# A transformer block's lead-in with three attention jobs' exponentials kept in SBUF, and seven units' second-norm transposes made by DMA

## The chip, the cores and the metric

The kernel runs on one core of a Trainium2 chip. A core has TensorE (PE; the load of its stationary operand is listed as PEld), VectorE (DVE), ScalarE (ACT), GpSimd (POOL) and SyncE (SP, which here only issues DMAs). Times are device microseconds of one execution. The time before is 1102.87 us, the median of three runs (1101.98 to 1104.28). In the profile, L12 is line 12 of the kernel before.

## The reference

A pre-norm transformer block on x of 2048 rows and 1024 columns in bf16, with 32 heads of 32 columns and a hidden layer of 3584. A layer norm here has no scale or shift.

```python
def _A_ref(x, wqkv, wo):
    B, S, D = x.shape
    H = 32; Dh = D // H
    qkv = (lambda x, *d: x.transpose(*d))((x @ wqkv).reshape(B, S, 3, H, Dh), 2, 0, 3, 1, 4)
    q, k, v = qkv[0], qkv[1], qkv[2]
    scale = Dh ** -0.5
    scores = jnp.einsum("bhqd,bhkd->bhqk", q, k) * scale
    p = _softmax(scores, axis=-1)
    o = jnp.einsum("bhqk,bhkd->bhqd", p, v)
    return (lambda x, *d: x.transpose(*d))(o, 0, 2, 1, 3).reshape(B, S, D) @ wo

def _B_ref(x, w1, b1, w2, b2):
    h = jnp.einsum("bsd,df->bsf", x, w1) + b1
    h = _gelu(h)
    return jnp.einsum("bsf,fd->bsd", h, w2) + b2

x = A_x
h = x + _A_ref(_layernorm(x, axis=-1), A_wqkv, A_wo)
h2 = h + _B_ref(_layernorm(h, axis=-1), B_w1, B_b1, B_w2, B_b2)
```

## The kernel before

**A planner writes the order.** The program first makes a list of tasks (`Graph.add`, L84). Each task has an engine, an occupation in us, a latency, a priority, and the buffers that it reads and writes, from which its dependences follow. `Graph.schedule` (L109) then plays the list through with these figures and writes down, for each engine, the order in which the tasks start. `assign` puts semaphores on what is left of the dependences and `emit` writes the instructions. On the chip every engine goes through its own list in that order and waits where a semaphore is not there yet. The planner's figures (L487 to L559: `MM`, `c_dve_ps`, `c_dve`, `c_act`, and the occupations and latencies in the calls) thus set the order and nothing else.

For TensorE `pick_pe` (L1144) chooses among the ready tasks by kind: scores (`qk`) go first; a value product (`pv`) or a denominator (`den`) is taken once `PV_FORCE` = 3 of them are ready, or when there is nothing else; otherwise the background work (`bg`) goes in the order of the list; `warm` is taken when there is nothing to do at all. On the other engines the task with the lowest priority number goes first.

**Attention.** The 32 heads are 8 groups g of four heads (128 columns). A job is one block qb of 256 query rows with one group g. It has eight rounds r of 256 keys. A round is: scores (`Att.qk`, L769: eight matmuls on quarters of the array's rows), two exponentials on ACT of 128x1024 elements (L779) from PSUM into one of nine buffers of `PT`, a sum of two halves on DVE into `PS` (L820), the value product (`Job.pv`, L805) and the denominator, a product with ones (`Job.den`, L834). The scores use PSUM in units of two banks; `n_units` says how many there are (three are banks 0 to 5). A job collects its output in one bank and `Job.finish` (L850 to L865) divides and stores it in `OT`.

**Order of the whole.**
- The lead-in: chunk hc of eight, two row tiles of 128 rows each, is loaded, normalized on DVE (`layer_norm`, L583 to L598), transposed by TensorE (L604) and copied from PSUM to `xnT` (L611 on ACT for most tiles, L613 on DVE). Then K of group 0 (and, for the first two chunks, Q) and V of groups 0 and 1 (`proj_v`, cast in L706) for that chunk, and rounds of jobs (0,0) and (1,0) with `n_units` 2 and a lag of two rounds. Banks 4 and 7 take the background work there, 5 and 6 the two jobs' outputs. In these two jobs the denominators are made from `PT` directly, without the DVE sum.
- For g = 1 to 7: Q, K and the next groups' V projections (`rest_of_projections`, L1072) as background, and jobs (0,g) and (1,g); for g = 2 (`EXTRA`) also (2,g).
- Then the remaining jobs, block by block, with this background for unit u = 0 to 6 (a unit is 256 rows): output projection `wo` (L886), second layer norm `ln2` (L914), first FFN layer `ffn1` (L925) with the GELU in `gelu` (a tanh on ACT, L965), second FFN layer `ffn2` (L969). The order within a unit is `wo(u + 1)`, `ffn2(u, 0)`, `ln2(u + 1)`, `ffn2(u, 1)`, `ffn1(u + 1)`. Banks 6 and 7 go to background work and job outputs.
- The tail: unit 7's output projection, norm and FFN, behind the last job.

At the start 80 `warm` matmuls (L1007) write bank 6. In `ln2`, each of the two tiles is normalized into `xb` (L598), transposed by eight matmuls into a PSUM bank (L604) and copied to `hnT` (L613; by ACT, L611, in the tail). The call is:

```python
            transposes(R.xb[:, s, :], R.B_xb[s], slot(), hnT[:, :, t * P:(t + 1) * P], B_hnT[t],
                       "act" if tail else "dve", 0)
```

All DMAs are issued by SP, in the planner's order. Weights come into rings: four blocks of 512 KB for the first layer (`w1r`), seven for the second (`w2r`).

## Time and profile before

| what | value |
|---|---|
| median of three runs | 1102.87 us |
| the profiled execution, first to last instruction | 1099.2 us |
| TensorE busy (its ends are modelled) | 1056.5 us |
| ACT busy | 1019.8 us, of which 1024 exponentials (L779) 953.6 |
| DVE busy | 757.2 us |
| transposes by TensorE outside the tail (L604) | 128 for xnT, busy 9.7 us; 112 for hnT, busy 9.0 us |
| copies to hnT by DVE (L613) | 14, 9.4 us |
| copies to xnT by ACT (L611) | 12, 12.2 us |
| DMA share over the span, main queue | 51.2% |

The profiled execution is one run of its own; its span counts from its first to its last instruction and lies 3.7 us under the median of the timed runs. A busy time is the union of an engine's instructions. "Idle before" is the time an engine stood still just before a group of instructions, with what released it. The chain that ended last is followed back from the last instruction, at each step to what released it or to the instruction before it on its engine.

### The profile page before, as it was taken

The page shows a single profiled execution, that of the slowest core. Times are in us where ns is not written, and L with a number is a line of the kernel's source. Part 1 is how long each engine was busy: PE and PEld are TensorE (multiplying, and loading weights), DVE is VectorE, ACT ScalarE, POOL GpSimd, SP SyncE. Part 2 cuts the span into 40 slices and gives each one's busy share as a digit, 9 for nine tenths or more (in the row PEclk, how much of TensorE's full clock was granted, in tenths as well). Part 3 has the DMA queues.
Part 4 walks back from the last instruction along what each step waited for, and adds up shares of the span by engine and source line. Part 5 has one row for each costly group of instructions (what it writes and reads, how often), then busy time and mean ns, then how long its engine had stood idle before and what let it go on. Part 6 is the DMA issues. An engine that isn't in the chain of part 4 may idle for free.

```text
span 1099.2 us, 42056 instructions
## 1 busy us (share of the span) xinstructions
PE 1056.5 (96%) x19177; PEld 613.8 (56%) x19226; DVE 757.2 (69%) x1444; ACT 1019.8 (93%) x1124; POOL 47.8 (4%) x110
## 2 busy tenths in 40 slices
PE   8899999998899999999999899999999999999998
PEld 6655555553345744664475456546744664565483
DVE  7746666665676886788588768876886787687501
ACT  3879999999999999999999999999999999999650
POOL 3200000000000001001000100010010000000100
PEclk9999999999899999999999999999999999999999
DMA  6820000048345654854576466448654747797370
GB/s 184 227 103 2 29 2 3 2 159 268 115 122 154 189 151 150 260 162 149 185 228 188 150 203 180 143 150 255 181 178 149 216 142 239 243 266 242 98 262 20
DMA packets 265506, 174.43 MB, mean 159 GB/s; under 512 B 26864, under 2 KB 260336, under 8 KB 264560
## 3 DMA queue, kind: packets, MB, share of 16 engines
q1 hardware_dynamic: 265328, 171.74, 51.2%
q8 instruction: 151, 2.47, 0.9%
q14 instruction: 27, 0.22, 0.1%
HBM read 161.23 MB, written 10.49 MB: 156 GB/s over the span
## 4 chain that ended last, share of the span: by engine, by line
ACT 79%; PE 19%; DVE 1%; issue 0%; DMA 0%; POOL 0%; POOLq 0%; DVEq 0%
ACT PT L779 75%; PE ps L540 6%; ACT uu L965 4%; PE ps L537 4%; PE ps L534 3%; PE ps L769 2%; PE ps L805 1%; PE ps L1007 1%; PE ps L834 1%; DMA a_w1r<-in_A_wo_dram 0%; ACT xnT L611 0%; PE ps L604 0%; DVE PS L820 0%; DVE OD L850 0%; DVE OD L857 0%
## 5 line engine op out<-in xcount | busy, mean ns | idle before, releaser
L779 ACT ACTIVATE PT<-ps 128x1024 bf16<-128x1024 f32 x1024 | 953.6, 1189 | 18.2 <-PE ps L769 18.0
L820 DVE TENSOR_TENSOR PS<-PT 128x1024 bf16<-128x1024 bf16 x434 | 287.5, 686 | 124.5 <-ACT PT L779 63.8
L769 PE MATMUL ps<-QT,KT 32*128 32x256 bf16 x4096 | 204.6, 273 | 13.5 <-ACT PT L779 10.2
L805 PE MATMUL ps<-PT,V 128*32 128x256 bf16 x4096 | 179.9, 273 | 1.5 <-ACT PT L779 1.1
L769 PEld LDWEIGHTS ps<-QT,KT 32*128 32x128 bf16 x4096 | 61.0, 92 | 174.1 <-ACT PT L779 165.3
L834 PE MATMUL ps<-PS,ones 128*32 128x256 bf16 x1736 | 121.7, 274 | 2.0 <-DVE PS L820 2.0
L805 PEld LDWEIGHTS ps<-PT,V 128*32 128x32 bf16 x4096 | 103.8, 97 | 30.0 <-issue 8.7
L537 PE MATMUL ps<-a_w2r,gT 128*128 128x512 bf16 x445 | 109.6, 380 | 4.9 <-issue 2.4
L537 PE MATMUL ps<-hnT,a_w1r 128*128 128x256 bf16 x903 | 111.2, 273 | 1.1 <-DVE rr L860 0.5
L534 PE MATMUL ps<-hnT,a_w1r 128*32 128x256 bf16 x2660 | 96.9, 274 | 2.4 <-DVE gT L943 1.2
L537 PEld LDWEIGHTS ps<-hnT,a_w1r 128*128 128x128 bf16 x903 | 82.7, 98 | 25.1 <-issue 14.8
L943 DVE TENSOR_TENSOR gT<-ps,b1f 128x512 bf16<-128x512 f32 x98 | 67.3, 687 | 27.7 <-PE ps L534 18.4
L534 PE MATMUL ps<-a_w2r,gT 128*32 128x512 bf16 x1140 | 81.6, 381 | 2.5 <-DVE OD L857 2.5
L534 PEld LDWEIGHTS ps<-hnT,a_w1r 128*32 128x32 bf16 x2660 | 66.2, 96 | 18.5 <-issue 14.0
L537 PEld LDWEIGHTS ps<-a_w2r,gT 128*128 128x128 bf16 x471 | 40.4, 98 | 55.3 <-issue 15.7
L989 DVE SCALAR_TENSOR_TENSOR hch<-ps,hch 128x512 bf16<-128x512 f32 x32 | 22.0, 689 | 64.0 <-PE ps L540 47.1
L834 PEld LDWEIGHTS ps<-PS,ones 128*32 128x32 bf16 x1736 | 45.9, 96 | 22.8 <-issue 8.7
L965 ACT ACTIVATE uu<-uu 128x1024 bf16<-128x1024 bf16 x49 | 58.0, 1206 | 0.0
L537 PE MATMUL ps<-xnT,Wall 128*128 128x512 bf16 (+1 forms) x213 | 47.7, 360 | 2.3 <-issue 1.1
L588 POOL CAST mvb<-mv 128x2 bf16<-128x2 f32 (+1 forms) x25 | 6.1, 242 | 990.0 <-DVE mv L585 987.2
L706 DVE CAST V<-ps 128x512 bf16<-128x512 f32 x32 | 22.1, 690 | 30.8 <-PE ps L537 15.8
L537 PE MATMUL ps<-Wall,xnT 128*128 128x256 bf16 x327 | 41.0, 273 | 0.0
(85 smaller groups left out, 1009.8 us busy)
## 6 DMA issues: line engine op xcount, KB each, us to landing
a_w2r<-in_B_w_dram SPq DMA_DIRECT2D x105, 512.0 KB, 5.6
a_w1r<-in_B_w_dram SPq DMA_DIRECT2D x98, 512.0 KB, 4.4
a_w1r<-in_A_wo_dram SPq DMA_DIRECT2D x32, 512.0 KB, 4.0
b_w1r<-in_B_w_dram SPq DMA_DIRECT2D x14, 512.0 KB, 5.8
a_w1r<-in_A_wqkv_dram SPq DMA_DIRECT2D x11, 512.0 KB, 4.3
xrb<-in_A_x_dram SPq DMA_DIRECT2D x16, 256.0 KB, 4.2
Wall<-in_A_wqkv_dram SPq DMA_DIRECT2D x16, 256.0 KB, 4.8
hch<-in_A_x_dram SPq DMA_DIRECT2D x16, 256.0 KB, 4.0
```

Of the source, the lines that this page charges most:

```text
L534: fns.append(lambda p, j=j: p.matmul(psum[32 * j:32 * j + 32, bi(bank), c0:c1], lhsT[:, 32 * j:32 * j + 32], rhs, start=start, stop=stop, ...
L537: t.whole = lambda p: p.matmul(psum[:, bi(bank), c0:c1], lhsT, rhs, start=start, stop=stop, skip_group_check=True)
L540: t = pe(lambda p: p.matmul(psum[:, bi(bank), c0:c1], lhsT, rhs, start=start, stop=stop), occ, reads=reads, writes=[bb(bank)], mode="full" ...
L706: t = dve(lambda v: v.tensor_copy(dst, psum[:, bi(bank), :].rearrange("p (t g c) -> p g t c", t=2, g=2)), c_dve_ps(512), reads=[bb(bank)], ...
L769: return p.matmul(psum[:, 2 * us[h // 2] + h % 2, 256 * i:256 * i + 256], KT[32 * h:32 * h + 32, g, k0:k0 + P], QT[32 * h:32 * h + 32, qs, :],
L779: act(lambda a, u=u, k=k: a.activation(PT[:, s, k, :, :], psum[:, 2 * u:2 * u + 2, :], ACT.Exp, bias=0.0, scale=SCALE), 1024, reads=[B_ps[ ...
L805: fns.append(lambda p, i=i, h=h: p.matmul(psum[32 * h:32 * h + 32, bi(bank), 0:256], V[:, g, 2 * r + i, 32 * h:32 * h + 32], PT[:, s, h // ...
L820: dve(lambda v: v.tensor_tensor(PS[:, n, :, :], pairs[:, :, 0:256], pairs[:, :, 256:512], ALU.add), c_dve(1024, 2), reads=[B_PT[2 * s], B_ ...
L834: fns.append(lambda p, h=h, rhs=rhs, i=i: p.matmul(psum[32 * h:32 * h + 32, bi(bank), 256:512], ones32[:, :], rhs, start=False, stop=last, ...
L943: t = dve(lambda v: v.tensor_tensor(g[:, fc:fc + 2, :], psum[:, bi(bank), :].rearrange("p (f c) -> p f c", f=2), b1f[:, fc:fc + 2].unsquee ...
L965: act(lambda a: a.activation(w, w, ACT.Tanh, bias=0.0, scale=KT2), 1024, reads=[B_uu[i]], writes=[B_uu[i]], prio=-1)
L989: drop(dve(lambda v, hs=hs, bank=bank, half=half: v.scalar_tensor_tensor(hch[:, hs, c], psum[:, bi(bank), :], half, hch[:, hs, c], ALU.mul ...
```

## The change

Four things change together.

1. **The lead-in.** Scores and exponentials of three jobs, (0,0), (1,0) and (2,0), run in the lead-in (`NLJ = 3`), with three units from the start. Their 24 rounds of exponentials each get a buffer of their own: eight of the nine of `PT` are used, and 16 more (`extra_pt`) lie over memory that is not yet in use there (K and V of groups 2 to 5, V of group 1, three of the weight blocks, and a piece behind them). V of group 0 is projected after all of this (`proj_v1`, four times four tiles), and the value products of the three jobs come behind it: the planner counts none of them as ready until the last cast of that V (`gate`) is done. They use the DVE sum as all others do, and those sums come after the last DVE task of the lead-in (`hold`). ACT copies only tiles 0 to 3 to `xnT`; DVE copies the other twelve. All background work uses banks 6 and 7, bank 6 from the end of the warm matmuls on. V of group 1 is projected in the stage g = 1.
2. **One more extra job.** `EXTRA` is now (1, 2), and the loops behind it follow.
3. **The second layer norm's transposes** of units 0 to 6 are made by one DMA for each tile of 128x1024, from `xb` to `hnT`, both in SBUF, issued by SP. Unit 7 keeps TensorE and ACT.
4. **The planner's figures** for matmuls, DVE and ACT instructions, latencies and switches are others.

The loads of V's weights are cut differently: 128 columns at first, behind the first eight row tiles, and the other 384 in one piece later.

```diff
+    PTs = [PT[:, i] for i in range(NR)]
+    B_PTs = [B_PT[2 * i:2 * i + 2] for i in range(NR)]
...
+    def extra_pt(off):
+        i = len(PTs)
+        h, b = sb(Area(off), "PX%d" % i, [P, 2, 2, 512], BF, 2)
+        PTs.append(h)
+        B_PTs.append(b)
+
+    for g in (2, 3, 4, 5):
+        extra_pt(B_KT[8 * g].lo)
+        extra_pt(B_V[NT * g].lo)
+    for k in (5, 3, 1):
+        extra_pt(B_W[k][0].lo)
+        extra_pt(B_W[k][0].lo + 4096)
+    extra_pt(ph0.cur)
+    extra_pt(B_V[NT].lo)
...
-    MM = 0.2195
+    MM = 0.21333
     def c_dve_ps(n):
-        return (120 + n) / 960.0 + 0.02
+        return (120 + n) / 960.0 - 0.058
 
     def c_dve(n, x=1):
-        return (62 + n / x) / 960.0 + 0.085
+        return (62 + n / x) / 960.0
...
     def pe(fns, occ, reads=(), writes=(), kind="bg", mode="full", prio=0, after=()):
-        return gr.add(E.PE, fns, occ, 0.16, reads, writes, prio, kind, mode, after)
+        return gr.add(E.PE, fns, occ, 0.225 if isinstance(fns, list) and len(fns) > 1 else 0.2, reads, writes, prio, kind, mode, after)
...
     def lead_slot():
-        s = Slot(gr.buf(), 1, (4, 7))
-        s.buf.over.append(B_ps[4])
-        B_ps[4].over.append(s.buf)
-        lead_slots.append(s)
-        return s
+        return slot()
...
+    def dma_transpose(out_ap, in_ap, nbytes, reads, writes, prio):
+        return gr.add(E.SP, lambda s: s.dma_start_transpose(out_ap, in_ap), 0.06, 0.0, reads, writes, prio, nbytes=2 * nbytes)
...
-            transposes(R.xb[:, s, :], R.B_xb[s], slot(), hnT[:, :, t * P:(t + 1) * P], B_hnT[t],
-                       "act" if tail else "dve", 0)
+            if tail:
+                transposes(R.xb[:, s, :], R.B_xb[s], slot(), hnT[:, :, t * P:(t + 1) * P], B_hnT[t], "act", 0)
+            else:
+                dma_transpose(hnT[:, :, t * P:(t + 1) * P], R.xb[:, s, :], P * 2048, [R.B_xb[s]], [B_hnT[t]], -1)
...
-            if r == 7 or (self.g == 0 and self.qb < 2):
+            if r == 7:
                 self.sums.append((s, True))
...
-    load_w(WV, -5, 0, 256)
     for tt in range(4, 8):
         x_tile(tt, -5)
+    load_w(WV, -5, 0, P)
     for k in range(80):
-        pe(lambda p: p.matmul(psum[:, 6, 0:256], ident[:, :], b2t[:, 0:256], start=True, stop=True), 0.12,
+        pe(lambda p: p.matmul(psum[:, 6, 0:256], ident[:, :], b2t[:, 0:256], start=True, stop=True), 0.18 if k < 42 else 0.115,
            reads=[B_ident, B_b2t], writes=[B_ps[6]], kind="warm")
-    LEAD_LAG = 2
-    lead_jobs = [Job(0, 0, 6), Job(1, 0, 5)]
-
-    att.n_units = 2
+    LEAD_ACT = (0, 1, 2, 3)
+    NLJ = 3
+    last_x = []
...
-            tr_tile(tt, lead_slot(), "dve" if tt >= 8 and tt % 2 else "act")
+            tr_tile(tt, slot(), "act" if tt in LEAD_ACT else "dve")
...
+        if hc < NLJ:
+            proj_half(0, hc, slot(), ev)
+        proj_half(1, hc, slot(), ev)
         if hc < 7:
             lead_norm(hc + 1)
-        proj_v(2 * hc, 0, lead_slot(), ev, first)
-        for k, r in {0: [(0, 0)], 1: [(0, 1), (1, 0), (1, 1)]}.get(hc, [(0, hc), (1, hc)]):
-            s = att.qk((k, 0), r)
-            pending.append((lead_jobs[k], r, s))
-            attention_drain(LEAD_LAG)
-    attention_drain()
-    att.n_units = 3
-    att.unit = 0
-    N_LEAD = sum(t.kind == "pv" for t in gr.tasks)
-    pool_banks = {4: [], 7: [], 6: [t for t in gr.tasks if any(t in x.w or t in x.r for x in (B_ps[6], B_psD[6]))]}
+        for k, r in [(k, hc) for k in range(min(hc, NLJ))] + ([(hc, r) for r in range(hc + 1)] if hc < NLJ else []):
+            n = 8 * k + r
+            s = NR + 15 if n == 0 else n - 1 if n < 9 else n
+            lead_rounds.append((k, r, att.qk((k, 0), r, s)))
+    att.rounds = 8
+    hold = [t for t in gr.tasks if t.eng == E.DVE][-1:]
+    for c in range(4):
+        proj_v1(4 * c, 0, 4, slot(), "dve", 0, True)
+    gate = gr.tasks[-1]
+    for k in range(NLJ):
+        job = Job(k, 0, slot(2))
+        for _, r, s in [x for x in lead_rounds if x[0] == k]:
+            job.pv(r, s)
+    pool_banks = {6: [t for t in gr.tasks if t.kind == "warm"][-1:], 7: []}
...
+        if g == 1:
+            for c in range(4):
+                proj_v1(4 * c, 1, 4, slot(), "dve", 0, True, [gate])
+        if g in EXTRA:
+            proj(0, g, 1, slot(), "dve")
...
-    EXTRA = [2]
+    EXTRA = [1, 2]
     for g in range(1, G):
         rest_of_projections(g)
-        if g in EXTRA:
-            proj(0, g, 1, slot(), "dve")
+        if g == 2:
+            proj(0, 0, 1, slot(), "dve")
...
-    attention(2, [g for g in range(G) if g not in EXTRA])
+    attention(2, [g for g in range(1, G) if g not in EXTRA])
...
+        if gate.done is None or gate.done > now + 1e-9:
+            return 0
...
-        if pv_next[0] < N_LEAD:
-            waiting += PV_FORCE - 1
```

More of the change, by code (lines that the diff above doesn't have):

```diff
@@ L708, in proj_v, with proj_v1 @@
         drop(t, bank)
-    def proj_v1(tt, g, n, bank, evac, c0=0):
+    def proj_v1(tt, g, n, bank, evac, c0=0, narrow=False, after=()):
         for k in range(n):
@@ L715, in proj_v1 @@
                 mm(bank, xnT[:, tc, dc, t4 * P:(t4 + 1) * P], Wall[4][:, dc, P * g:P * g + P], dc == 0, dc == DC - 1,
[L716 removed]
+                   [B_W[4][g], B_xnTt[tc][t4]], narrow, cols=(c0 + P * k, c0 + P * k + P), after=after)
         dst = V[:, g, tt:tt + n, :]
@@ L754, in __init__, with qk @@
             self.jobs = 0
-        def qk(self, job, r):
+        def qk(self, job, r, s=None):
             qb, g = job
@@ L849, in finish @@
             D = OD[:, o, 1, :].rearrange("p (b j) -> p b j", j=32)
-            t = dve(lambda v: v.transpose(OD[:, o, 1, :], psum[:, bi(bank), 256:512]), 0.445,
+            t = dve(lambda v: v.transpose(OD[:, o, 1, :], psum[:, bi(bank), 256:512]), 0.36,
                     reads=[self.B_O, self.B_D], writes=B_D, prio=-1)
@@ L1097, in build_kernel @@
             attention(2, [g])
-    for g in range(2):
+    for g in range(1, 2):
         if g not in EXTRA:
@@ L1126, in build_kernel @@
     pvs = [t for t in gr.tasks if t.kind == "pv"]
-    pv_exp = [[d for d in t.deps if d.eng == E.Activation and d.kind == "exp"] for t in pvs]
+    pv_exp = [[d for d in t.deps if d.eng == E.Activation and d.kind == "exp" or d.eng == E.DVE] for t in pvs]
     pv_next = [0]
@@ L1146, in pick_pe @@
         spare = None
+        ready_rounds(now)
         n67 = sum(b > 5 for b in free)
```

58 lines of the change are left out of this document (27 added, 31 removed).

## The prediction

> **What bounds the kernel now.** I read the page first, then the busy time by stage, then what ScalarE (ACT) waited for in the lead-in and behind it, then ACT's instructions in order of time. The page:
>
> ```profile
> PE 1056.5 (96%) x19177; PEld 613.8 (56%) x19226; DVE 757.2 (69%) x1444; ACT 1019.8 (93%) x1124; POOL 47.8 (4%) x110
> ...
> ACT 79%; PE 19%; DVE 1%; issue 0%; DMA 0%; POOL 0%; POOLq 0%; DVEq 0%
> ```
>
> Two engines look full. TensorE's 96% is modelled, and the chain that ended last runs through ACT for 79% of the span. By stage (width, then busy time and count of PE, PEld, DVE, ACT, POOL, then the clock and the DMA share):
>
> ```profile
> 24.80:71.21 46.41, 42.03 (x1032) 29.43 (x1033) 29.75 (x67) 35.88 (x38) 7.95 (x17) 1.00 0.70 201
> 71.21:279.50 208.29, 200.09 (x3674) 111.09 (x3687) 129.50 (x234) 208.29 (x228) 0.00 (x0) 1.00 0.20 65
> ...
> 1031.00:1099.20 68.20, 64.77 (x434) 40.29 (x439) 11.49 (x23) 19.43 (x37) 3.40 (x8) 1.00 0.37 125
> ```
>
> From 71.2 on ACT is busy without a break: 228 exponentials in 208.29 us, 0.914 us each. The last one ends at 1031.1; the 68.1 us behind it are TensorE's (the last unit's output projection and two FFN layers). So the time is the moment at which ACT becomes continuous, plus ACT's remaining work, plus 68. ACT's waits, in the lead-in (16 to 72 us) and then from 71 to 1031:
>
> ```profile
> ACT PT L779 <- PE ps L769: 15.0, 12, 3.8
> ...
> ACT PT L779 <- PE ps L769: 6.7, 5, 3.6
> ```
>
> Behind 71 us only 6.7 us are to be had from ACT; in the lead-in there is more:
>
> ```profile
> 24.82 1.02 ACT L779 ACTIVATE PT<-ps 128x1024 bf16<-128x1024 f32 x1 [3.82 <-PE ps L769]
> 25.73 2.85 ACT L611 ACTIVATE xnT<-ps 128x1024 bf16<-128x1024 bf16 x3
> ...
> 57.58 1.94 ACT L779 ACTIVATE PT<-ps 128x1024 bf16<-128x1024 f32 x2 [0.55 <-PE ps L769]
> 60.09 1.94 ACT L779 ACTIVATE PT<-ps 128x1024 bf16<-128x1024 f32 x2 [0.58 <-PE ps L769]
> 63.12 1.94 ACT L779 ACTIVATE PT<-ps 128x1024 bf16<-128x1024 f32 x2 [1.08 <-PE ps L769]
> 65.63 1.94 ACT L779 ACTIVATE PT<-ps 128x1024 bf16<-128x1024 f32 x2 [0.57 <-PE ps L769]
> 71.21 4.69 ACT L779 ACTIVATE PT<-ps 128x1024 bf16<-128x1024 f32 x5 [3.65 <-PE ps L769]
> ```
>
> Every pair of exponentials waits about 0.55 us: the lead-in uses two PSUM units, a round fills both, so the next round's scores (L769) cannot be written until this round's are read. Besides, ACT copies normalized tiles (L611), and at 71.2 it waits 3.65 us for the next group's first projections.
>
> **The lead-in.** By 71.21 ACT has done 32 exponentials. Between 24.8 and 71.2 it did 30 of them, eight L611 copies (8 x 1.03 = 8.2 us) and was idle for 46.41 - 35.88 = 10.5 us. The change takes all three causes away: only tiles 0 to 3 are copied by ACT, scores go round three units, and 24 rounds (48 exponentials) are on offer before group 1 is needed. If ACT runs without a break from the second chunk's first exponential, which I put at 24.0 (24.8 before; V's eight-matmul fillers and a V cast are gone ahead of it, but the 80 warm matmuls now hold bank 6 until the last has run), the 33rd starts at 24.0 + 30 x 0.914 = 51.4. That is 19.8 us before 71.21 (10.5 idle, 8.2 copies, 0.8 start, rounding). Bounds for the start: 22 (two tiles' copies right behind each other) to 27 (one bank serialises the second chunk, three copies of 1.0 more).
>
> Can it be fed? VectorE (DVE) has, over the lead-in, 21.2 us of L583, 3.3 of L585 (16 of 32), 8.0 of L598, 1.1 of L589, twelve xnT copies at 0.69 = 8.3, and ten casts of 128x256 at 0.42 = 4.2: 46 us from 3.4 on, done near 50. The seven later chunks offer 3, 5, 3, 3, 3, 3, 3 rounds, so ACT wants chunk 7 only at 24 + 20 rounds x 1.83 = 60.6, chunk 2 at 29.5 (before, its K cast came at 28.8 with V casts in between). TensorE per chunk: 16 transposes (1.0 us), eight to sixteen 256-wide matmuls (0.9 to 1.8), three rounds (0.33 each): under 4 us of 5.5. So ACT sets the pace, and I book 19.8.
>
> **The handover, at a cost of 2 us.** V of group 0 (64 narrow 128-column matmuls, 3.6 us, and four casts of 0.69) and all 24 value products come after the scores, behind the gate (the last V cast), near 53. They cost TensorE 24 x (0.22 + 0.11) = 8 us and DVE 21 sums x 0.69 = 14.5 us, while group 1's first Q and K (16 matmuls, 3.5 us, two casts) must be there at 66 to 68, when ACT has used up its 24 rounds. The planner prefers a value product as long as three are ready, so the projections stand behind that burst unless they were fitted in before; their weights landed at 33 to 35 us before, so mostly they can be. Nothing hidden: 0; hidden by nothing: the 8 us of the burst. I take 2. The loads of the second halves of W wait for the third job's value products, about 75 us, and are wanted beyond 110: no cost. Score rounds of group 1 write buffers that job 0's products must have read; those run first.
>
> **One more Q projection and 16 more rounds ahead of group 2.** ACT's total stays. TensorE gets 8 x 0.219 us earlier. Two jobs' sums now go through DVE (14 x 0.69) and TensorE saves 14 x 0.11 = 1.5 us. Nothing on the path: DVE is 69% busy.
>
> **The planner's figures.** They move the order, not a duration. With ACT's waits behind 71 us at 6.7, the best is -6.7; the worst is a stretch in which ACT waits for TensorE as at 279 to 286 (1.5 us), a handful of times: +5. I take 0.
>
> **The DMA transposes, at nothing.** Out go 112 TensorE transposes (8 per tile, 0.056 apart: 6.3 us) and 14 DVE copies of 0.68 (9.4 us). Neither bounds that stretch. In come 14 DMAs on SP's queue, behind DVE's L598, ahead of weight loads whose ring slots wait for TensorE anyway. An issue on SP takes about 0.4 us. The cover is the other half of the FFN's second layer, which stands between. The narrowest is unit 6:
>
> ```profile
> 938.71 0.54 DVE L598 TENSOR_SCALAR a_xb<-hch,mvr,rden 128x1024 bf16<-128x1024 bf16 x1
> ...
> 956.19 1.25 PE L537 MATMUL ps<-hnT,a_w1r 128*128 128x256 bf16 x10 [0.16 <-DVE rr L860]
> ```
>
> 16.9 us from the normalized tile to its first reader; units 1 to 5 have 26 to 30. No transposing DMA is in the trace. Nearest rows for 256 KB:
>
> ```profile
> hch<-in_A_x_dram SPq DMA_DIRECT2D x16, 256.0 KB, 4.0
> ...
> b1b<-in_B_b_dram SPq DMA_DIRECT2D x1, 7.0 KB, 8.6
> ```
>
> 4.0 us if it moves like a load of that size; and if it moved element by element like the strided gather of b1b (3,584 elements), (8.6 - 3.1 of b2t) / 3,584 = 1.5 ns each, 131,072 would take about 200 us. It is a dedicated operation of that size on whole rows, so I take the first, 4 to 10 us with loads ahead of it in the queue, all hidden. The Trainium skill speaks against the change: "VectorE: DVE Perf Modes", The three transpose paths, gives 1309 ns for 128x128 by DMA and 390 ns by TensorE, and advises TensorE where PSUM will do. The trace has TensorE's eight at 0.6 us a tile; by the page's figure eight blocks would take an estimated 10.5 us a tile, two in a row 21, which by unit 6's 16.9 us (the first tile starts 6 us earlier) is still just covered, so the sum would not move. "DMA: Bandwidth & Descriptors", Latency and other measured facts, has 261 GB/s, an estimated 1 us; no run here shows either yet.
>
> **The sum.** 19.8 - 2 = 17.8, less 1.3 for the odd wait inside 24 rounds = 16.5 us. Span 1099.2 - 16.5 = 1082.7. The runs' median, 1102.87, lies 3.7 above the profiled span, and I carry that: **1086 us**. A run is told from no change at about 0.2%, 2.2 us.
>
> **Rivals.**
> *TensorE does not follow.* ACT's last exponential comes 16.5 us sooner, but TensorE's remaining work shrinks only by the transposes and sums, 7.8 us; then the tail grows by 8.7: 1099.2 - 7.8 + 3.7 = 1095. For: 96% busy, and half a second-layer block (28 matmuls) was already done ahead of the tail, so little was left over. Against: from 250 to 286 PE was busy 29.85 of 36, in the lead-in 42.03 of 46.41, and the matmuls' counted columns (0.2192 us per 512, as in the tail, where 49 take 10.74 us) fill 625 of the 745 us from 286 to 1031; 377 rounds with two switches of tiling at 0.115 (the gap between groups of matmuls there) are 87; some 33 us of waits remain, and 8.7 are needed.
> *The burst starves group 1.* The whole 8 us: 1086 + 6 = 1092 to 1094. For: the 3.65 us wait at 71.2 is this handover, before. Against: free TensorE time from 33 us on.
> *The lead-in is not freed,* another pace (DVE, one bank) holds the rounds, and only the eight copies leave ACT: -8.2, 1095.
> *Slower: transposes late.* Place: the first matmul on hnT of units 0 to 6, in TensorE's order ahead of the scores, so ACT stops too. It decides once a pair of tiles lands 16.5 / 7 = 2.4 us later than its cover, i.e. at 28 to 30 us in units 1 to 5. At the b1b row's rate a pair takes 400: 7 x (400 - 26) = 2,600 us, about 3,700 in all. For: no such DMA in the trace, and the DMA share from 855 to 955 is 0.64 already. Against: all other rows of 64 to 1,024 KB land in 3 to 8 us.
>
> **Chances.** Forecast 0.60 (its own range 1079 to 1091: start 22 to 27, handover 0 to 8, ±5 behind). TensorE 0.17, burst 0.10, not freed 0.05, late transposes 0.08. Faster by over 0.2%: 0.88 (the first four, less a little for their sum); within 0.2%: 0.04; slower: 0.08. Range: down to 1078 (start at 22, no handover cost, 3 of the 6.7 us), up to 1096, which takes in the next three cases and leaves out the late transposes.
>
> **What would show it.** ACT without a break from about 24 to beyond 110, its 33rd exponential near 51; L611 four xnT copies; last exponential near 1014 and 68 us behind it (77 if TensorE lags). A hole in ACT at 60 to 75 is the burst; a wait of L534 or L537 for a DMA onto hnT is the transpose. Wrong would be: the 33rd exponential behind 60, or a tail over 72.

## The result, and the profile after

The changed kernel takes 1092.74 us (median of four runs, 1089.33 to 1094.19) against 1103.57 us for the kernel before on the same chip: a ratio of 0.9905, 95% interval 0.9877 to 0.9934, so 0.7 to 1.2% faster. The prediction said 1086, within 1078 to 1096. The profiled execution spans 1090.2 us, 9.0 us less than before. In the new file the lines have moved: scores are L784 (L769 before), exponentials L795 (L779), value products L821, denominators L850; L546, L549 and L552 are the matmuls of the background work.

The page of the changed kernel, first the busy times, then the chain that ended last:

```profile
PE 1045.6 (96%) x19048; PEld 609.6 (56%) x19107; DVE 755.9 (69%) x1453; ACT 1014.5 (93%) x1116; POOL 43.4 (4%) x110
...
PE 54%; ACT 39%; DVE 5%; issue 1%; DMA 1%; SPq 0%; POOL 0%; POOLq 0%; DVEq 0%
```

Before, the chain was ACT's for 79% of the span and TensorE's for 19%; now TensorE has more of it than ACT. ACT has the same 1024 exponentials and only eight copies fewer: the chain leaves ACT where an exponential waited for its scores, and then stays with TensorE until something released that.

ACT's instructions in order of time, from the lead-in to the last long stretch (start, length, count, and in brackets the idle time before, with what ended it):

```profile
22.91 3.77 ACT L795 ACTIVATE PT<-ps 128x1024 bf16<-128x1024 f32 x4 [2.99 <-PE ps L784]
...
30.32 7.45 ACT L795 ACTIVATE PX<-ps 128x1024 bf16<-128x1024 f32 x8
...
50.51 3.86 ACT L795 ACTIVATE PX<-ps 128x1024 bf16<-128x1024 f32 x4
...
65.06 7.65 ACT L795 ACTIVATE PT<-ps 128x1024 bf16<-128x1024 f32 x8
76.51 197.17 ACT L795 ACTIVATE PT<-ps 128x1024 bf16<-128x1024 f32 x214 [3.80 <-PE ps L784]
...
276.83 15.01 ACT L795 ACTIVATE PT<-ps 128x1024 bf16<-128x1024 f32 x16 [1.03 <-PE ps L784]
...
434.64 28.72 ACT L795 ACTIVATE PT<-ps 128x1024 bf16<-128x1024 f32 x31 [1.46 <-PE ps L784]
...
817.74 28.83 ACT L795 ACTIVATE PT<-ps 128x1024 bf16<-128x1024 f32 x31 [1.47 <-PE ps L784]
```

From 22.91 to 72.7 there is no hole: the pairs of the lead-in and their half microsecond between pairs are gone, and the row that starts at 50.51 begins with the 33rd exponential (71.21 before). The first hole comes with the 57th, at 76.51. Then come waits of half a microsecond to one and a half which the kernel before did not have in that number. All of ACT's longer waits from 71 to 1022 us:

```profile
ACT PT L795 <- PE ps L784: 11.3, 11, 3.8
```

Eleven waits, 11.3 us, where there were five and 6.7. Without the handover (3.8 here, 3.6 before) that leaves 7.5 against 3.1 us.

By stage (width; busy time and count of PE, PEld, DVE, ACT, POOL; clock; DMA share and GB/s):

```profile
24.80:72.70 47.90, 42.68 (x781) 28.47 (x782) 43.11 (x88) 47.90 (x53) 7.29 (x16) 1.00 0.47 150
72.70:76.50 3.80, 3.37 (x22) 1.43 (x24) 3.55 (x11) 0.01 (x1) 0.00 (x0) 1.00 1.04 235
```

ACT is full in the lead-in (47.90 of 47.90; 35.88 of 46.41 before) and empty in the 3.8 us behind it.

**An account of the 9.0 us.** ACT's steady pace is 0.9136 us for an exponential and 0.9375 for a tanh. Take an exponential's start and subtract what all exponentials and tanhs ahead of it cost at this pace: the rest is the time by which ACT is late there, its lag. At the 57th exponential (56 ahead) the lag went from 42.0 to 25.3 us, a gain of 16.7. From there to the last exponential the lag grew by 7.4 us before and by 14.9 now: call it the slip. The end of the last exponential is at 1021.9 (1031.1 before), and the tail behind it has 68.3 us (68.1). So 16.7 - 7.5 - 0.2 = 9.0. The lead-in brought what was booked, and almost half of it was lost over the next 950 us. By the medians the change is 10.8 us: the profiled execution of the kernel before lies 4.4 us under its median on this chip, that of the changed kernel 2.6 us under.

### The profile page after: what moved, and what is told of

It reads as the page before. It is cut to its first block, busy times and chain, and to the rows that moved or that the text cites. A ratio compares the mean times of both kernels' runs of the same rounds, so it can differ in the third digit from the quotient of the medians.

```text
span 1090.2 us, 41817 instructions
## 1 busy us (share of the span) xinstructions
PE 1045.6 (96%) x19048; PEld 609.6 (56%) x19107; DVE 755.9 (69%) x1453; ACT 1014.5 (93%) x1116; POOL 43.4 (4%) x110
## 4 chain that ended last, share of the span: by engine, by line
PE 54%; ACT 39%; DVE 5%; issue 1%; DMA 1%; SPq 0%; POOL 0%; POOLq 0%; DVEq 0%
ACT PT L795 35%; PE ps L549 18%; PE ps L546 12%; PE ps L784 8%; PE ps L821 6%; PE ps L552 5%; PE ps L850 3%; ACT PX L795 2%; DVE PS L836 2%; ACT uu L983 2%; DMA xrb<-in_A_x_dram 0%; DVE OD L866 0%; PE ps L1025 0%; SPq L570 0%; DVE OD L873 0%
## 5 line engine op out<-in xcount | busy, mean ns | idle before, releaser
L795 ACT ACTIVATE PT<-ps 128x1024 bf16<-128x1024 f32 x992 | 922.4, 1082 | 14.7 <-PE ps L784 14.3
L836 DVE TENSOR_TENSOR PS<-PT 128x1024 bf16<-128x1024 bf16 x434 | 286.6, 685 | 128.9 <-PE ps L850 68.1
L784 PE MATMUL ps<-QT,KT 32*128 32x256 bf16 x4096 | 205.3, 274 | 10.7 <-ACT PT L795 5.4
L821 PE MATMUL ps<-PT,V 128*32 128x256 bf16 x3968 | 174.4, 274 | 2.8 <-ACT PT L795 2.8
L784 PEld LDWEIGHTS ps<-QT,KT 32*128 32x128 bf16 x4096 | 61.2, 92 | 166.3 <-ACT PT L795 134.8
L850 PE MATMUL ps<-PS,ones 128*32 128x256 bf16 x1792 | 124.6, 275 | 4.8 <-DVE PS L836 4.0
L821 PEld LDWEIGHTS ps<-PT,V 128*32 128x32 bf16 x3968 | 102.1, 97 | 29.4 <-issue 6.8
L549 PE MATMUL ps<-hnT,a_w1r 128*128 128x256 bf16 x949 | 116.5, 274 | 1.1 <-DVE gT L961 0.5
L549 PEld LDWEIGHTS ps<-hnT,a_w1r 128*128 128x128 bf16 x949 | 87.9, 98 | 25.8 <-issue 14.5
L546 PE MATMUL ps<-a_w2r,gT 128*32 128x512 bf16 x1372 | 98.3, 381 | 0.4 <-DVE hch L1007 0.2
L549 PE MATMUL ps<-a_w2r,gT 128*128 128x512 bf16 x382 | 93.8, 380 | 4.2 <-issue 2.9
L546 PE MATMUL ps<-hnT,a_w1r 128*32 128x256 bf16 x2476 | 88.9, 274 | 4.0 <-issue 1.6
L546 PEld LDWEIGHTS ps<-hnT,a_w1r 128*32 128x32 bf16 x2476 | 60.4, 96 | 20.6 <-issue 16.8
L850 PEld LDWEIGHTS ps<-PS,ones 128*32 128x32 bf16 x1792 | 47.0, 96 | 30.7 <-DVE PS L836 14.2
L549 PEld LDWEIGHTS ps<-a_w2r,gT 128*128 128x128 bf16 x413 | 35.2, 98 | 47.4 <-issue 13.4
L549 PE MATMUL ps<-xnT,Wall 128*128 128x512 bf16 (+1 forms) x256 | 53.5, 344 | 4.5 <-DVE rr L876 2.8
L546 PEld LDWEIGHTS ps<-a_w2r,gT 128*32 128x32 bf16 x1372 | 30.0, 96 | 25.6 <-issue 14.0
L549 PE MATMUL ps<-Wall,xnT 128*128 128x128 bf16 (+1 forms) x443 | 43.9, 247 | 0.0
```

The lines of the kernel that those rows point to most:

```text
L546: fns.append(lambda p, j=j: p.matmul(psum[32 * j:32 * j + 32, bi(bank), c0:c1], lhsT[:, 32 * j:32 * j + 32], rhs, start=start, stop=stop, ...
L549: t.whole = lambda p: p.matmul(psum[:, bi(bank), c0:c1], lhsT, rhs, start=start, stop=stop, skip_group_check=True)
L784: return p.matmul(psum[:, 2 * us[h // 2] + h % 2, 256 * i:256 * i + 256], KT[32 * h:32 * h + 32, g, k0:k0 + P], QT[32 * h:32 * h + 32, qs, :],
L795: act(lambda a, u=u, k=k: a.activation(PTs[s][:, k, :, :], psum[:, 2 * u:2 * u + 2, :], ACT.Exp, bias=0.0, scale=SCALE), 1024, reads=[B_ps ...
L821: fns.append(lambda p, i=i, h=h: p.matmul(psum[32 * h:32 * h + 32, bi(bank), 0:256], V[:, g, 2 * r + i, 32 * h:32 * h + 32], PTs[s][:, h / ...
L836: dve(lambda v: v.tensor_tensor(PS[:, n, :, :], pairs[:, :, 0:256], pairs[:, :, 256:512], ALU.add), c_dve(1024, 2), reads=B_PTs[s], writes ...
```

## The experiments

Three theories were held against each other. **A**: TensorE has too little room, so that ACT's earlier start cannot be followed. **B**: the planner's new figures give an order in which scores come late; **B1** and **B2** blame one pair of figures each. **C**: the DMA transposes, or the traffic that goes with them, stand in the way. Each kernel's ratio is to the kernel before, on its own chip. The table gives the start of the 33rd and 57th exponential, the slip to the 273rd and to the last exponential, the tail, and the time between 60 and 1085 us at which the granted clock was at half; all from one profiled execution each, worked out from the start times. That execution is one of several: for e1, e3, e4 and e6 it was the slowest of its kernel, 2.2 to 3.6 us over the median.

```
kernel                        ratio [95%]              33rd  57th   slip 273rd / last  tail  half clock
before                        1                        71.2  93.2        2.6 /  7.4    68.1     6.8
changed                       0.9905 [0.9877, 0.9934]  50.5  76.5        3.0 / 14.9    68.3    13.7
e12 changed again             0.9926 [0.9907, 0.9945]  49.5  76.9        2.7 / 16.9    66.7    17.1
e1 without DMA transposes     0.9958 [0.9944, 0.9971]  49.3  77.0        3.2 / 17.8    72.8    13.7
e2 DMA transposes alone       1.0027 [1.0014, 1.0041]  70.9  92.8        2.7 / 10.9    68.3    27.3
e3 figures alone              1.0060 [1.0038, 1.0082]  70.9  92.9        3.7 / 17.4    68.7    30.7
e4 both of these              1.0085 [1.0067, 1.0102]  67.9  89.9        3.2 / 22.5    69.3    41.0
e5 changed, old figures       1.0083 [1.0067, 1.0098]  51.9  76.7       12.7 / 23.7    79.6    17.1
e6 changed, ACT's figure old  0.9985 [0.9972, 0.9997]  50.1  72.2        8.7 / 30.1    68.8    30.7
e7 changed, MM old            0.9928 [0.9914, 0.9943]  49.5  76.3        2.0 / 18.0    68.8     6.8
e8 changed, both of these     0.9933 [0.9911, 0.9954]  50.3  72.1        8.3 / 25.7    66.8    13.7
e9 changed, less TensorE work 0.9955 [0.9939, 0.9971]  49.8  77.1        2.0 / 19.3    69.0    47.8
e10 changed, fewer matmuls    0.9972 [0.9962, 0.9982]  49.7  77.3        5.3 / 21.7    68.3    23.9
e11 changed, K ahead          0.9933 [0.9920, 0.9947]  49.4  71.4       10.5 / 25.9    66.8    13.7
```

The changed kernel and its repetition show the spread between executions: 14.9 and 16.9 us of slip. Differences of 2 us in that column are no evidence.

### The parts: DMA transposes, figures, lead-in

e1 is the changed kernel with the transposes back on TensorE:

```diff
-            if tail:
-                transposes(R.xb[:, s, :], R.B_xb[s], slot(), hnT[:, :, t * P:(t + 1) * P], B_hnT[t], "act", 0)
-            else:
-                dma_transpose(hnT[:, :, t * P:(t + 1) * P], R.xb[:, s, :], P * 2048, [R.B_xb[s]], [B_hnT[t]], -1)
+            transposes(R.xb[:, s, :], R.B_xb[s], slot(), hnT[:, :, t * P:(t + 1) * P], B_hnT[t],
+                       "act" if tail else "dve", 0)
```

> The changed kernel with the second norm's transposes back on TensorE and DVE in all units. Behind the lead-in the changed kernel's ScalarE slips 15.0 us against its own work (7.5 before). Theory A (TensorE has no room left for the tighter order): 112 transposes, 6.3 us, more on TensorE, so the slip grows to 18 to 22 us and the time to 1095 to 1100. Theory B (the planner's new figures pack TensorE too tightly, whatever the amount): slip 15, 1091 to 1095. Theory C (the transposing DMAs get in the way): slip back to about 8, 1084 to 1088.

e2 is the kernel before with that edit made the other way round.

> The kernel before with only the 14 transposing DMAs. Theory A: ScalarE was continuous there, so TensorE's 6.3 us buy at most part of the 7.5 us of slip: 1098 to 1104. Theory B: the same. Theory C: the slip doubles, 1108 to 1112.

e3 is the kernel before with the planner's new figures, of which these are five:

```diff
-    MM = 0.2195
+    MM = 0.21333
...
-        return (120 + n) / 960.0 + 0.02
+        return (120 + n) / 960.0 - 0.058
...
-        return 0.073 + (0.093 if ap_bias else 0.0) + n / 1200.0
+        return (0.064 if n == 1024 else 0.073) + (0.093 if ap_bias else 0.0) + n / 1200.0
...
-        return gr.add(E.Activation, fn, c_act(n, ap_bias), 0.14, reads, writes, prio, kind, after=after)
+        return gr.add(E.Activation, fn, c_act(n, ap_bias), 0.16, reads, writes, prio, kind, after=after)
...
-        return gr.add(E.DVE, fn, occ, 0.08, reads, writes, prio)
+        return gr.add(E.DVE, fn, occ, 0.135, reads, writes, prio)
```

> The kernel before with only the planner's new figures. Theory A: no more work for TensorE and the same start of the continuous stretch, so the slip stays near 7.5 and the time within 1099 to 1106. Theory B: the slip goes up by 5 to 8 us as in the changed kernel: 1107 to 1112, unless the lead-in gains from the new order.

e4 is the kernel before with the edits of e2 and e3.

> The kernel before with the transposing DMAs and the new figures, so the changed kernel without its lead-in and second extra job. Theory A: 1098 to 1103. Theory B: 1106 to 1112. The difference to the changed kernel is the lead-in's worth: 16 to 17 us at the 56th exponential if the prediction's sum for the lead-in holds.

e5 is the changed kernel with all these figures back (only the cost of a switch stays at 0.104).

> The changed kernel with the planner's figures of before, but for the switch of tiling (0.104). The figures alone cost 0.6% on the kernel before and raised ScalarE's slip behind the lead-in from 7.5 to 17.4 us. Theory B (figures): the slip goes from 15.0 back to 7 to 10, the 56th exponential stays near 76, time 1084 to 1088. Theory A (TensorE is simply full now that ScalarE starts 17 us earlier): slip 13 to 17, 1090 to 1095.

Against these expectations: e1's time (1096.3) is the one that A asked for, with a slip just short of A's; e2 (1104.4) lies at the upper end of A's and B's and not by C; e3 (1108.0) and e4 (1111.6) lie in B's ranges; e5 (1111.9) lies in none. Between e4 and the changed kernel the 57th exponential moves by 13.4 us, not 16 to 17, because e4's own order had already brought 3.3.

Put in one table, the parts do not add:

| ratio to before | old lead-in, old figures | old lead-in, new figures | new lead-in, old figures | new lead-in, new figures |
|---|---|---|---|---|
| TensorE transposes | 1 | 1.0060 | not run | 0.9958 |
| DMA transposes | 1.0027 | 1.0085 | 1.0083 | 0.9905 (0.9926 on repetition) |

On the old lead-in the new figures cost 0.6%; on the new one they are worth 1.6 to 1.8% (1.0083 against 0.9926 and 0.9905). The new lead-in (always together with the second extra job; no run separates the two) is worth 1.6 to 1.8% with the new figures (against 1.0085) and makes the kernel 0.6% slower with the old ones (1.0083 against 1.0027). The DMA transposes cost 0.3% on the kernel before, and with the new figures there another 0.25%, which the two intervals do not tell from nothing; beside the new lead-in they bring 0.3 to 0.5%, of which the lower end is not clear of the intervals either. So B holds for the kernel before, where the figures alone give a slip like the changed kernel's (17.4), but the old figures are no cure: they make it 23.7.

What goes wrong in e5 is the handover. Its ACT in order of time:

```profile
74.86 5.63 ACT L795 ACTIVATE PT<-ps 128x1024 bf16<-128x1024 f32 x6 [1.35 <-PE ps L784]
88.31 5.61 ACT L795 ACTIVATE PT<-ps 128x1024 bf16<-128x1024 f32 x6 [7.83 <-PE ps L784]
```

and TensorE meanwhile:

```profile
80.16 0.39 PE L850 MATMUL ps<-PX,ones 128*32 128x256 bf16 x8
82.51 3.60 PE L546 MATMUL ps<-xnT,Wall 128*32 128x512 bf16 x32 [1.96 <-DVE OD L873]
85.90 1.81 PE L546 MATMUL ps<-Wall,xnT 128*32 128x128 bf16 x60
87.65 0.61 PE L784 MATMUL ps<-QT,KT 32*128 32x256 bf16 x8
```

TensorE waits 1.96 us for a job's output bank, then makes projections for 5.1 us in a row before the scores come: ACT idles 7.83. And e5's tail has 79.6 us instead of 68.3: background work was left over for the end (500 matmuls from the last exponential on, against 425).

**Theory C falls in its plain form.** The 14 transposes as the changed kernel's SP issued them (issue min/median/max in ns, first and last start in us), and their landing:

```profile
L575 SPq DMA_TRANSPOSE hnT<-a_xb x14: 1239/1294/3207, 307.9 to 933.1; - x14
...
DMA to landing us min/median/max: 2.7/3.7/6.5
```

No instruction in the trace waits for one. The narrowest place is unit 6, where the second tile landed 3.4 us ahead of its first reader (29 to 41 us in the other units); in e4 TensorE did wait there, 0.74 us. In e1 ACT slips as much (17.8) without them; what e1's profiled execution has lost against the changed kernel is mainly in the tail, 72.8 us, with 450 matmuls from the last exponential on against 425: work that came too late to be done beside ACT. This execution lies 3.6 us over e1's median, so how much of the tail the median has is not known. e2 has 3.5 us more slip than the kernel before, and its clock was at half for 27.3 us against 6.8; what each of order and clock cost was not separated. The last section shows the clock.

### Two figures, one at a time

```diff
-        return (0.064 if n == 1024 else 0.073) + (0.093 if ap_bias else 0.0) + n / 1200.0
+        return 0.073 + (0.093 if ap_bias else 0.0) + n / 1200.0
...
-        return gr.add(E.Activation, fn, c_act(n, ap_bias), 0.16, reads, writes, prio, kind, after=after)
+        return gr.add(E.Activation, fn, c_act(n, ap_bias), 0.14, reads, writes, prio, kind, after=after)
```

That is e6, on the changed kernel; e7 puts `MM` back to 0.2195 (and 0.0026 to 0.003); e8 does both.

> The changed kernel with only ScalarE's figures of before (an exponential counted 0.926 us, where the trace has 0.914; new 0.917). Theory B1 (the old surplus of 0.012 us on each exponential is what left TensorE its room): slip 7 to 10, 1084 to 1088. If the surplus is not it, 14 to 17 and 1091 to 1095.

> The changed kernel with only the matmul's figure of before (0.2225 us for 512 columns, where the tail has 0.2192; new 0.2159). Theory B2 (TensorE's background is counted 1.5% too short and runs late): slip 7 to 10, 1084 to 1088. If not, 14 to 17 and 1091 to 1095.

> Both of the two before. By B1 or B2 no worse than the better of them: slip 7 to 10, 1083 to 1088. Theory A: 1090 to 1095 in all four.

B1 falls: e6 is 0.6 to 0.8% slower than the changed kernel, with a slip of 30.1. B2 is not borne out: e7 has the time of the repetition (0.9928 and 0.9926), and its slip of 18.0 has another shape. 5.4 of it are one hole; ACT there, and TensorE just before it:

```profile
945.05 5.60 ACT L795 ACTIVATE PT<-ps 128x1024 bf16<-128x1024 f32 x6 [5.43 <-PE ps L821]
...
938.76 0.40 PE L784 MATMUL ps<-QT,KT 32*128 32x256 bf16 x8
939.08 5.58 PE L546 MATMUL ps<-a_w2r,gT 128*32 128x512 bf16 x100
```

Here the planner's list itself holds 100 quarter matmuls (25 whole ones cut in four) between two rounds of scores. Such an accident is what another figure changes; where it falls could not be told from the figure. e8 is 4.4 us better than the changed kernel at the 57th exponential and 6.4 us worse at the end; much of that lies at stops of TensorE for which the profile names no releaser (the split below).

### Is TensorE full?

e9 takes work from TensorE where it is said to be full: the second FFN layer of units 0 to 5 leaves out the last 4 of its 28 hidden blocks, 6 x 2 x 2 x 4 = 96 matmuls of 512 columns, 21 us at 0.2192.

```diff
-            for fc in range(FC):
+            nf = 24 if u < 6 else FC
+            for fc in range(nf):
...
-                mm(bank, gs[u][:, fc, t * P:(t + 1) * P], W.w2[:, s, fc % 4, :], fc == 0, fc == FC - 1,
+                mm(bank, gs[u][:, fc, t * P:(t + 1) * P], W.w2[:, s, fc % 4, :], fc == 0, fc == nf - 1,
```

> The changed kernel, but the second FFN layer of units 0 to 5 leaves out the last 4 of its 28 hidden blocks (96 matmuls of 512 columns, 21 us of TensorE's background; all loads stay). ScalarE's own work is the same. Theory A (TensorE is too full to have the scores ready in time): the slip behind the lead-in goes from 15 to 8 or less, the part of it with TensorE busy from 7.6 to 3 or less; about 1084 to 1086. Theory D (the slip is single holes, from the order and from the supply of instructions, not a lack of room): 12 to 17, 1089 to 1095.

Its windows (us, PE, PEld, DVE, ACT, POOL, clock, DMA share, GB/s):

```profile
993.00:1007.00 14.00, 12.49 (x304) 6.63 (x300) 8.06 (x15) 14.00 (x17) 0.00 (x0) 0.99 0.65 211
1007.00:1020.60 13.60, 10.28 (x156) 3.53 (x152) 5.68 (x11) 13.26 (x16) 0.00 (x0) 0.50 0.15 42
```

Theory A falls. With 21 us less to do TensorE did not bring scores sooner: the slip is 19.3, where A asked for 8 or less. From 277 to 1020 us TensorE is busy for 707.7 us, against 718.3 in the changed kernel: 10.6 us of the work taken away became idle time. Most of the rest went to the clock, which in that stretch was at half for 33.0 us against 6.8 (47.8 in all; the second row is one such stretch). Without the lag that grew in and just behind the slow stretches (7.9 us; 2.2 and 4.5 in the changed kernel's two executions) the slip is 11.4 against 12.7 and 12.4, so the clock does not hide a gain that A would explain. The kernel became 0.3 to 0.5% slower, with less to do. The expectation's theory D, single holes, asked for 12 to 17 us and at most 1095; the measured 19.3 and 1098.3 lie outside it as well.

e10 asks whether the number of instructions is the trouble (the supply of instructions stops at times, below). Runs of quarter matmuls are merged to whole ones from 0.5 us on, not from 3.0:

```diff
-            if k == 0 or sum(x.occ for x in run[k:]) >= 3.0:
+            if k == 0 or sum(x.occ for x in run[k:]) >= 0.5:
```

> The changed kernel with the same order; only runs of narrow matmuls of 0.5 us or more (before: 3.0) are issued as whole ones, which takes 1575 matmuls and as many weight loads, 7.5% of all instructions, out of TensorE's stream. If TensorE's stops with the profile's word issue (4.2 us of ScalarE's slip) come from its supply of instructions, they shrink to 2 to 4 us, 1089 to 1093; if not, nothing moves but the switches of tiling: 1092 to 1096.

The order is the same, with 1575 weight loads fewer. The stops became fewer: behind the 57th exponential TensorE stood still with the word issue (it waited for nothing that the profile shows) for more than 0.4 us twice (1.5 us in all), against six and five times (4.7 and 3.2 us) in the changed kernel's two executions. Yet the slip is 21.7 and the kernel is 0.5 to 0.7% slower than the changed one, outside both of the ranges given. What it has more of is switches between whole and quartered matmuls: 1128 against 1028, an estimated 11.5 us of TensorE at the prediction's 0.115 each. That these switches are the reason was not tried.

### The hole at the handover

TensorE of the changed kernel at the hole of 3.80 us:

```profile
70.55 0.39 PE L850 MATMUL ps<-PX,ones 128*32 128x256 bf16 x8
73.13 3.00 PE L549 MATMUL ps<-xnT,Wall 128*128 128x512 bf16 x13 [2.19 <-DVE rr L876]
76.06 0.40 PE L784 MATMUL ps<-QT,KT 32*128 32x256 bf16 x8
```

It waits 2.19 us until DVE is done with a job (L876), then makes K for 3.0 us, then scores. Only banks 6 and 7 serve background and job outputs, and the third job had taken the second one while K of group 1 was still to come. e11 puts Q and K of group 1 ahead of the third job's value products:

```diff
+    proj(0, 1, 0, slot(), "dve", direct=True)
+    for tc in range(4):
+        proj(1, 1, tc, slot(), "dve")
+    khold = gr.tasks[-1:]
+    for k in range(NLJ):
+        job = Job(k, 0, slot(2))
+        job.after = khold if k in (2,) else ()
```

> The changed kernel with K and Q of group 1 listed ahead of the value products of the lead-in's jobs, and the third job's first value product behind the last K cast of group 1. If the hole of 3.8 us in ScalarE at 72.7 is the second bank taken by the third job while K waits for it, the 56th exponential comes at 72.5 to 73.5 instead of 76.5. With the rest as in the changed kernel 1087 to 1091; if what follows lands on another order with more slip, up to 1096. If the bank is not it, the hole stays within 1 us of 3.8.

Its ACT, and its TensorE (in this file L822 is the value product):

```profile
63.97 13.14 ACT L795 ACTIVATE PT<-ps 128x1024 bf16<-128x1024 f32 x14
78.99 3.77 ACT L795 ACTIVATE PT<-ps 128x1024 bf16<-128x1024 f32 x4 [1.87 <-PE ps L784]
87.21 1.94 ACT L795 ACTIVATE PT<-ps 128x1024 bf16<-128x1024 f32 x2 [4.45 <-PE ps L822]
```

```profile
77.50 0.46 PE L546 MATMUL ps<-Wall,xnT 128*32 128x128 bf16 x19 [1.77 <-issue]
...
82.42 2.08 PE L546 MATMUL ps<-Wall,xnT 128*32 128x128 bf16 x136
84.33 0.38 PE L822 MATMUL ps<-PT,V 128*32 128x256 bf16 x5
86.87 0.61 PE L822 MATMUL ps<-PT,V 128*32 128x256 bf16 x11 [2.16 <-issue]
```

The cause is shown as far as the order goes: with K first the hole is gone and the 57th exponential starts at 71.4, not 76.5. e11 moves the third job's products and its bank together, so it does not tell the bank from the products; for the bank speaks that TensorE stood idle for 2.19 of the 3.80 us, which a burst of products would not do.

The gain is not kept: at the 273rd exponential the lag is 30.8 us, against 28.3 and 28.5 in the changed kernel's two executions. Part of this is work that the handover owes: from 82.4 TensorE makes projections for 2.1 us before the value products that ACT's next exponential waits for. But of the 6.3 us of ACT's two waits shown, 3.9 are the two rows marked issue, where TensorE stood still for 1.77 and 2.16 us and nothing in the profile released it. e6 and e8, whose figures also close the hole, come to 29.8 and 29.2, and e8 has such a stop of 2.64 us at 87.8. So in these executions closing the hole brought nothing that lasted; what it would bring without those stops is not shown.

### The changed kernel once more

> The changed kernel once more, to see which of the holes in ScalarE behind the lead-in belong to the order and which to the execution. If they belong to the order: the same 11 waits within a microsecond of the same places (76.5, 276.8, 434.6, 592.9, 766.6, 817.7, 865.6), slip 14 to 16, time 1090 to 1094. If the longer ones (434.6 and 817.7, where TensorE stands still with the profile's word issue) come from the supply of instructions in that execution, these two move or vanish and others come, slip 12 to 18.

1093.71 us, ratio 0.9926. Its ACT:

```profile
76.90 196.95 ACT L795 ACTIVATE PT<-ps 128x1024 bf16<-128x1024 f32 x214 [5.21 <-PE ps L784]
...
435.90 28.72 ACT L795 ACTIVATE PT<-ps 128x1024 bf16<-128x1024 f32 x31 [0.65 <-PE ps L784]
...
560.02 1.02 ACT L795 ACTIVATE PT<-ps 128x1024 bf16<-128x1024 f32 x1 [1.06 <-PE ps L784]
...
819.12 28.77 ACT L795 ACTIVATE PT<-ps 128x1024 bf16<-128x1024 f32 x31 [0.55 <-PE ps L784]
```

The holes ahead of the stretches of 31 come back, at 0.65 and 0.55 us where the first execution had 1.46 and 1.47: the place belongs to the order, some 0.9 us of the length to the execution. The hole at 560 is new here; e10, with the same order, has one of 1.08 us at 562.9. There are 17 waits with 14.1 us in place of 11 with 11.3, and the slip of 16.9 lies above the 14 to 16 expected for the order alone.

**What the slip is made of.** The growth of the lag can be sorted by place: at exponentials that start between the beginning of a stop of TensorE over 0.4 us with the word issue and 3 us behind its end; at those in a slow stretch of the clock or within 2.5 us behind it; and the rest.

| us | slip | at stops | slow clock | rest |
|---|---|---|---|---|
| before | 7.4 | 1.3 | 2.0 | 4.1 |
| changed | 14.9 | 5.5 | 2.2 | 7.2 |
| e12 changed again | 16.9 | 4.1 | 4.5 | 8.3 |
| e8 changed, both figures old | 25.7 | 15.4 | 3.8 | 6.5 |
| e10 changed, fewer matmuls | 21.7 | 2.1 | 5.0 | 14.6 |
| e11 changed, K ahead | 25.9 | 13.4 | 4.4 | 8.1 |

Of the 7.5 us by which the changed kernel slips more than the kernel before, 4.2 lie at stops, 0.2 at the slow clock and 3.1 elsewhere; on repetition 2.8, 2.5 and 4.2 of 9.5. This sorts by place; an exponential near a stop need not be late because of it.

**What stays open.** In every run with the new lead-in the slip is 15 to 30 us, against 7.4 in the kernel before; apart from the holes shown above it lies mostly in waits under 2 us, scattered over 950 us. That it comes with the order is shown (e3 makes it with figures alone, which change no work). The slow clock alone is not it: e7 was at half for 6.8 us, as the kernel before, and slipped by 18.0. Which property of an order decides is open: no single figure, no hole at the handover and no shortage of TensorE time in all accounts for it, the stops account for a part, and no version tried beats the changed kernel.

## Why the prediction was right, and where it was off

Faster was right, and the time lies in the range; the forecast of 1086 was 6.7 us too low. The forecast's own range ended at 1091, and the time of 1092.7 lies beyond it: the whole range holds it only because it was drawn out to 1096 for rivals that did not come about. That part is luck. The lead-in, which the forecast rests on, came as it was summed up.

- **"The lead-in", 19.8.** Right. The 33rd exponential came at 50.5, booked for 51.4. The second chunk's exponentials start at 22.91 (24.0 was taken, from 22 to 27), four xnT copies are left on ACT, and ACT sets the pace: it has no hole until 72.7. The "odd wait" booked at 1.3 was about 0.5: 54 exponentials from 22.91 end at 72.2 at the steady pace, and at 72.7 in the trace.
- **"The handover, at a cost of 2 us".** 3.8, and 5.2 on repetition, within the 0 to 8 given; by the trace for another reason than the one written. TensorE did not work off a burst of value products there but stood idle for 2.19 us until a job was done and its bank free, and then made K. With all this the gain at the 57th exponential is 16.7, and the sum had 16.5.
- **"The planner's figures. They move the order, not a duration ... I take 0", worst +5.** This is the step that failed: it is the term for all of ACT's waits behind the lead-in, taken at 0 and at +5 at worst. Behind the handover ACT gave back 14.9 us (16.9 on repetition), 7.5 to 9.5 more than before, so the last exponential ended at 1021.9 and not near 1014. The bound was made from one kind of long wait, a handful of them; the loss came as more waits of half a microsecond to one and a half (7.5 us against 3.1 in the waits that the profile lists) and as shorter ones. The sum had no term for TensorE's stops, at which 5.5 us of the slip lie (1.3 before). And the planner's figures were priced as a term of their own, though they have no price of their own: they cost 0.6% on the old lead-in and bring 1.6 to 1.8% on the new one.
- **"The DMA transposes, at nothing".** 2.7 to 6.5 us to landing (4 to 10 was taken), nobody waits. In unit 6, though, 3.4 us were left. The issue takes SP 1.24 to 3.2 us, not 0.4, without consequence here. The Trainium skill ("VectorE: DVE Perf Modes", The three transpose paths) gives 1309 ns for 128x128 by DMA, from which 10.5 us for a tile had been estimated: the trace does not agree with that estimate, its median is 3.7 for eight blocks, so here the figure does not go up with the number of blocks. "At nothing" holds for waiting; as an edit it cost 0.3% alone and brought 0.3 to 0.5% beside the new lead-in.
- **"TensorE does not follow", 1095.** The time came near, the mechanism did not: the tail is 68.3, not 77, and e9 shows that TensorE's room in all is not what is short. With the old figures (e5, tail 79.6) the long tail does appear.
- **"The burst starves group 1", 1092 to 1094.** Again the time without the mechanism: that hole has 3.8 of the 8 us. e5 has it at 7.83.
- **"The lead-in is not freed" and "transposes late"** did not occur.

## What to carry to other kernels

When a planner writes the order, price a change together with the order that comes with it: here each of three parts makes the kernel slower in one company and faster in another, so run the combinations before naming a part good or bad. Follow the lag of the bounding engine against its own steady pace at several points of the span: it shows at once whether a gain was never made, was given back at one hole, or leaked away. A hole closed at one place is worth only what is left of it two hundred microseconds later. And before a late engine is put down to the work in its way, see whether that engine worked at all just before: some of the holes here are TensorE standing still with nothing to wait for.

## What the hardware showed

**TensorE's clock halves without a long stop.** The kernel before, in the 15.6 us ahead of a slow stretch, and in it:

```profile
262.00:277.60 15.60, 13.01 (x255) 5.90 (x248) 8.53 (x17) 15.60 (x18) 0.00 (x0) 1.00 0.83 253
277.60:284.40 6.80, 5.51 (x33) 1.57 (x34) 3.42 (x8) 6.04 (x8) 0.00 (x0) 0.50 0.05 14
```

TensorE was busy for 13.01 of 15.6 us, its longest stop there was 0.49 us, and then the clock was at 0.50 for 6.8 us. In e9 it was the same, with 12.49 of 14 and 0.42 us ahead of 13.6 us at half. The place goes with the kernel: in all 14 traces one slow stretch begins between 267 and 287 us. The total lies from 6.8 to 47.8 us over these traces, always near a multiple of 3.4, and it grew when TensorE had less to do: all five runs of e9 have a mean granted clock of 0.978 to 0.983, the ten of the changed kernel 0.987 to 0.995. The Trainium skill, "TensorE: Matmul & The Clock Gate", HAM oscillation, gives "no PE-idle gaps >~3.4µs" as the rule; the trace does not agree, since no gap was over 0.49. The section behind it, A second HAM failure mode, has frequent short idling do the same, and these rows are in line with that.

**TensorE stops at fixed places for its instructions.** In the changed kernel, between the third and fourth of eight matmuls of one round of scores, and the same two groups on repetition:

```profile
815.54 0.28 PE L784 MATMUL ps<-QT,KT 32*128 32x256 bf16 x3
817.32 0.39 PE L784 MATMUL ps<-QT,KT 32*128 32x256 bf16 x5 [1.49 <-issue]
...
817.85 0.28 PE L784 MATMUL ps<-QT,KT 32*128 32x256 bf16 x3
818.70 0.39 PE L784 MATMUL ps<-QT,KT 32*128 32x256 bf16 x5 [0.57 <-issue]
```

Nothing in the profile ends these waits, and the weight loads stand still with the matmuls. The page of the changed kernel has a queue of its own for instructions:

```profile
q8 instruction: 150, 2.46, 0.9%
```

Its 150 packets are 16 KB each. On repetition, also with 150 packets, the trace has 38,394 instructions of TensorE: one packet for 256 of them. In the five traces that hold as many matmuls as weight loads (e5 to e8 and e12) 25 of the 26 stops over 0.4 us come behind 193 to 195 instructions of a block of 256. And in all 14 traces each of the 47 stops over 0.7 us (up to 2.64) has a packet of that queue that began 2.17 to 2.64 us before TensorE went on; a moment taken at random has one 2.1 to 2.8 us ahead in about one case of ten. So TensorE waits there for its next block of instructions.

Where it can happen goes with the order: of the changed kernel's six stops over 0.4 us four come again at the same instructions on repetition (434, 747, 817 and 864 us). How long it takes goes with the execution: 1.23, 0.60, 1.49 and 0.41 us there, 0.42, 0.53, 0.57 and 0.44 here. Traffic goes with it but is not needed: of the 45 stops over 0.7 us behind 60 us, 22 had a DMA share of 0.99 or more in the 4 us ahead, which a tenth to a sixth of all such stretches have, and 11 had under 0.7. What makes one block late and not the next is not shown.
